# A Performer attention and MLP-mixer kernel on one core: token-mix tails in column tiles, key tails by two heads, eight single PSUM banks

## The chip, the cores and the metric

The kernel runs on one core of one Trainium2 chip. The metric is the time of one execution on the device in microseconds (us). TensorE (PE) does the matmuls and writes PSUM; VectorE (DVE) and ScalarE (ACT) read PSUM and do the element-wise work; GpSimd (POOL) works on SBUF and issues DMAs; SyncE (SP) issues DMAs. PEld is TensorE's loading of weights, which overlaps its matmuls.

## The reference

Eight samples with eight heads of 64 dimensions and 576 tokens go through attention with 128 random features, and the result through an MLP mixer. Cut to what matters:

```python
def phi(x):                                   # x is q or k, scaled by D ** -0.25
    proj = einsum('bhsd,md->bhsm', x, omega)  # 128 features
    h = proj - sum(x * x, -1, keepdims=True) / 2
    return exp(h - max(h, -1, keepdims=True)) / sqrt(m)
kv  = einsum('bhsm,bhsd->bhmd', k_p, v);  z = sum(k_p, axis=2)
num = einsum('bhsm,bhmd->bhsd', q_p, kv)
den = einsum('bhsm,bhm->bhs', q_p, z)[..., None] + 1e-6
x   = num / den                               # then [8, 576, 512]
h   = maximum(x.T @ w_tok1, 0) @ w_tok2       # token mix, over 576 tokens
u   = x + h.T
out = u + maximum(u @ w_ch1, 0) @ w_ch2       # channel mix, 512 -> 1536 -> 512
```

## The kernel before

**Tiling.** A sample's 576 tokens are 512 main tokens in four blocks of 128 and a tail of 64. Everything on TensorE is in fp16. The tails are handled apart from the main part, since 64 tokens fill only half of 128 rows.

**Loading.** Samples 0 and 1 are loaded in their natural layout and transposed on TensorE. For samples 2 to 7, `load_transposed` (L351) has POOL issue one DMA for q and one for k, each of which converts a whole sample to fp16 in a DRAM scratch (L355), and SP issue a transposing DMA for each from the scratch to SBUF (`qT`, `kT`, L363). The q and k casts of sample b wait for `touch(b-2)`: a one-column POOL copy (L373) that reads the transposed mixer input `uT` of sample b-2, and so waits until this other transposing DMA (L762) has landed. After `kT` has landed, a POOL copy (L366) moves the key tails of all heads into the tile `ktt`. The main load of v (L335) waits for that copy; v's tails (`vt`, L344, two DMAs) are issued after the casts. DMAs that POOL issues keep the order in which they stand in the code.

**Attention.** The contraction over 64 dimensions uses half of the array's rows, so two tokens' sets are computed on the two row halves. For each of the four head pairs of a sample: `kp` (L617) and `qp` (L631) project keys and queries, ACT takes their exponentials (L500), DVE takes the keys' maxima and their reciprocals (L643, L645), POOL scales v by them (`vs`, L650), `kv` (L663) sums keys times values over the main tokens with a column for z, and `num` (L698, L700) multiplies queries with it. DVE then divides (L707, L708), which gives `x`.

**Tails of k.** `kt` (L532) projects them for all heads. In the 128 rows of one tile of `kpt` lie 32 tokens of each of four heads, in two tiles for even and odd tokens. So that a head gets only its own rows, `vbd` holds v's tails in a block-diagonal form with a mask of four columns: DVE writes the scaled mask (L568), POOL multiplies it with v's tails (L577, 128 x 1024 elements). For each head pair two matmuls of 130 columns (L670), one for even and one for odd tokens, add the tails to `kv`.

**PSUM.** It is divided into six single banks and one pair of banks. The pair serves the projected tails of k and q (L532, L592), whose exponentials are one ACT instruction over both banks, and in samples 2 to 7 the numerators of two heads, which DVE then divides by one reciprocal and one multiplication. Samples 0 and 1 use single banks for the numerators, one head at a time.

**Mixer.** `token_mix` (L730) computes for each sample two blocks of token features over all 512 channels (L737, L738), a ReLU on ACT or DVE (L743, L745), and the four main token blocks (L754), to which DVE adds x (L757). Sample 0 has its own form (L770). `token_tail` (L807) computes the 64 tail tokens of two samples together: `w2t` holds the tail columns of the second weight padded to 128 with zeros, once in the left half and once in the right, so that four matmuls of 512 columns with 128 output rows put one sample's tail in rows 0 to 63 and the other's in rows 64 to 127 (L813). POOL fills `w2t` by two copies at the start (L900). `channel_mix` (L823) computes twelve blocks of four matmuls (L832), each with a ReLU (L852), then four output blocks of twelve matmuls (L870), an addition on DVE (L879) and a store. All tails are one ninth group of 512 rows at the end.

**Order.** It is written by a planner in the kernel itself (`Planner`, L38), which runs when the program is built. Each piece of work is a job with an engine, a cost, a key, the jobs that it depends on, and the buffers it takes and gives back. The planner simulates the engines, and lets an engine that is free take, among the jobs that can start first, the one with the lowest key; a job with `rows=True` (half-row matmuls) after another of its kind gets the bonus `ks`, and a change between half rows and whole rows is given a cost of 0.1. The keys of sample b are b plus the entries of `KEYS` and `NEAR`; those of the first sample are written out in `HEAD`. The order is fixed in the program: each engine works through its list, and waits at each item for its inputs. Until the first channel-mix matmul, the planner also fills gaps of TensorE with warm-up matmuls on zeros (L925).

## Time and profile before

| | |
|---|---|
| Median of 6 runs | 291.25 us (290.91 to 291.52) |
| The profiled execution | 291.58 us, of which the span from first to last instruction 289.8 us |
| Granted TensorE clock, mean | 0.999 |
| Busy: PE, PEld | 283.1 us (98%), 143.1 us (49%) |
| Busy: DVE, ACT, POOL | 147.9 us (51%), 153.1 us (53%), 90.9 us (31%) |
| Channel mix on PE: L832 and L870, all shapes | 376 + 48 + 444 matmuls |
| Tails of the token mix, L813 | 16 matmuls |
| k's tails into kv, L670 | 64 matmuls |
| DMA | 75737 packets, 39.57 MB |

The page gives for each group of instructions the line, the engine, the operation, what it writes and reads, how often it occurs, its busy time and the mean of one, and the idle time of its engine before it with what ended that. The mean of a matmul there (379 ns for 512 columns) is from start to modelled end and overlaps the next one; what one costs in a full stream is seen from the steps between starts, as in the chain of work that ended last or in the timeline. A digit of the row PE is the busy share of one of 40 slices of the span, 9 being 90% or more.

### The profile page before, as it was taken

What the parts mean: (1) busy time and instruction counts of PE and PEld (TensorE: products, weight loads), DVE (VectorE), ACT (ScalarE), POOL (GpSimd) and SP (SyncE); (2) the same over time, 40 slices, a digit from 0 to 9 for tenths busy, and PEclk for the clock granted to TensorE, in tenths of its full rate; (3) what the DMA queues carried; (4) which work ended last, traced back from release to release, by engine and by line L of the source; (5) the groups of instructions that cost most, each with busy time, mean ns of one, the idle gap of its engine ahead of it and who ended that gap; (6) DMA issues with size and microseconds to landing.
All of it is one profiled execution on the core that took longest, in us unless ns stands there. A gap on an engine that the chain in (4) does not pass through costs nothing.

```text
span 289.8 us, 5517 instructions
## 1 busy us (share of the span) xinstructions
PE 283.1 (98%) x2207; PEld 143.1 (49%) x2207; DVE 147.9 (51%) x280; ACT 153.1 (53%) x307; POOL 90.9 (31%) x116
## 2 busy tenths in 40 slices
PE   7999999999999999999999999999999999999994
PEld 4576454445544544464445444554455444444442
DVE  3985974476469524854657246646565231111012
ACT  2993981198367554855466646653765402512600
POOL 8995930247017401740274016501431000000000
PEclk9999999999999999999999999999999999999999
DMA  8999999899975997989868976998511043013014
GB/s 186 189 184 194 202 224 180 150 219 176 160 123 143 194 117 145 183 190 196 96 153 164 205 100 109 193 197 127 122 74 38 0 92 127 0 46 116 2 35 110
DMA packets 75737, 39.57 MB, mean 137 GB/s; under 512 B 54976, under 2 KB 70720, under 8 KB 75328
## 3 DMA queue, kind: packets, MB, share of 16 engines
q0 software_dynamic: 24304, 17.43, 41.3%
q1 hardware_dynamic: 50624, 21.01, 33.8%
q10 hardware_dynamic: 784, 0.79, 0.8%
q8 instruction: 17, 0.28, 0.4%
q14 instruction: 8, 0.07, 0.1%
HBM read 35.88 MB, written 16.52 MB: 181 GB/s over the span
## 4 chain that ended last, share of the span: by engine, by line
PE 92%; ACT 3%; DMA 2%; issue 0%; ACTq 0%; DVE 0%; DVEq 0%
PE bank L870 33%; PE bank L832 31%; PE bank L737 4%; PE bank L754 4%; PE bank L617 3%; PE bank L663 3%; PE bank L631 2%; PE pair L698 2%; DMA wc<-in_k_dram 2%; ACT kp L500 1%; PE bank L813 1%; PE bank L670 1%; PE bank L471 1%; PE bank L738 1%; ACT qp L500 1%; PE bank L781 1%
## 5 line engine op out<-in xcount | busy, mean ns | idle before, releaser
L870 PE MATMUL bank<-wc,r 128*128 128x512 f16 (+2 forms) x444 | 101.5, 374 | 0.0
L852 ACT ACTIVATE r<-bank 128x512 f16<-128x512 f32 x106 | 63.3, 601 | 70.4 <-PE bank L832 69.8
L832 PE MATMUL bank<-uT,wc 128*128 128x512 f16 x376 | 90.1, 379 | 0.3 <-ACT kp L500 0.2
L870 PEld LDWEIGHTS <-r 128*128 128x128 f16 x444 | 40.4, 98 | 47.5 <-issue 5.1
L832 PEld LDWEIGHTS <-wc 128*128 128x128 f16 x424 | 39.3, 98 | 42.4 <-issue 1.2
L500 ACT ACTIVATE qp<-bank 128x512 f16<-128x512 f32 x64 | 35.6, 622 | 13.9 <-PE bank L631 13.8
L643 DVE TENSOR_REDUCE km<-kp 128x8 f16<-128x1024 f16 x32 | 38.6, 1207 | 7.7 <-ACT kp L500 7.7
L500 ACT ACTIVATE kp<-bank 128x512 f16<-128x512 f32 x64 | 34.3, 609 | 10.6 <-PE bank L617 10.6
L650 POOL TENSOR_TENSOR vs<-v,vs 128x512 f16<-128x512 f16 x32 | 33.5, 1057 | 15.4 <-DVE vs L645 11.8
L879 DVE TENSOR_TENSOR o<-u,bank 128x512 f32<-128x512 f16 x28 | 19.1, 681 | 28.1 <-PE bank L870 28.1
L757 DVE TENSOR_TENSOR u<-x,bank 128x512 f16<-128x512 f16 x28 | 17.4, 681 | 9.1 <-PE bank L754 9.1
L577 POOL TENSOR_TENSOR vbd<-vt,vbd 128x1024 f16<-128x1024 f16 x7 | 13.5, 1928 | 25.9 <-DVE vbd L568 18.1
L366 POOL COPY ktt<-kT 128x256 f16<-128x256 f16 x6 | 2.4, 398 | 59.1 <-DMA kT<-k 59.1
L708 DVE TENSOR_TENSOR x<-pair,rc 128x640 f16<-128x640 f32 x24 | 19.8, 824 | 0.8
L707 DVE RECIPROCAL rc<-pair 128x10 f32<-128x10 f32 x24 | 5.1, 214 | 22.4 <-PE pair L700 22.4
L698 PEld LDWEIGHTS <-qp 128*128 128x128 f16 x256 | 12.9, 98 | 6.1 <-issue 0.4
L745 DVE TENSOR_SCALAR r<-bank 128x512 f16<-128x512 f32 x7 | 4.8, 692 | 19.1 <-PE bank L738 19.1
L737 PE MATMUL bank<-x,w1m 128*128 128x512 f16 x56 | 14.4, 379 | 0.0
L663 PEld LDWEIGHTS <-kp 128*128 128x128 f16 x256 | 11.0, 98 | 5.4 <-ACT qp L500 0.6
L663 PE MATMUL bank<-vs,kp 128*128 128x65 f16 x256 | 13.0, 193 | 0.4 <-ACT qp L500 0.4
L754 PE MATMUL bank<-r,w 128*128 128x512 f16 x56 | 13.2, 379 | 0.0
L617 PE MATMUL bank<-omT,kT 64*128 64x128 f16 x256 | 12.1, 218 | 0.0
(109 smaller groups left out, 276.3 us busy)
## 6 DMA issues: line engine op xcount, KB each, us to landing
out_dram<-o SPq DMA_DIRECT2D x32, 256.0 KB, 2.5
q<-in_q_dram POOLq DMA_DIRECT2D x6, 576.0 KB, 6.7
k<-in_k_dram POOLq DMA_DIRECT2D x6, 576.0 KB, 10.0
wc<-in_moe_w_ch_dram POOLq DMA_DIRECT2D x4, 768.0 KB, 10.7
v<-in_v_dram POOLq DMA_DIRECT2D x6, 512.0 KB, 6.0
r<-in_q_dram POOLq DMA_DIRECT2D x4, 256.0 KB, 7.7
v<-in_v_dram POOLq DMA_DIRECT2D x4, 256.0 KB, 7.6
out_dram<-o SPq DMA_DIRECT2D x5, 128.0 KB, 2.4
```

Source lines behind the costliest of these rows:

```text
L500: nc.scalar.activation(out=out, in_=in_, func=AF.Exp, bias=0.0, scale=1.0)
L617: nc.tensor.matmul(ps[e][:, c : c + M], m[half[e], r, :], omT[half[e]], start=True, stop=True)
L643: nc.vector.reduce_max(out=mx, in_=kpv, axis=AX.X)
L650: nc.gpsimd.tensor_tensor(out=vs[:, :, 0:D], in0=t_v[place("v", b)][:, hh[0] : hh[0] + 2, :].rearrange("p h (j d) -> p (h j) d", d=D), in1 ...
L663: nc.tensor.matmul(ps[:, i, :], kpv[:, 2 * i + j // 2, j % 2, :], vs[:, i * NJ + j, 0 : D + 1], start=(i == 0 and j == 0), stop=False, ski ...
L708: nc.vector.tensor_tensor(out=t_x[place("x", b)][:, :, (2 * hp + hs[0]) * D : (2 * hp + hs[0] + n) * D].rearrange("p j (i d) -> p i j d", ...
L737: nc.tensor.matmul(ps, w1m[:, j, tb * P : (tb + 1) * P], x[:, j, :], start=(j == 0), stop=False)
L754: nc.tensor.matmul(ps, w2_of(tb, j), r1[:, tb, :], start=(tb == 0), stop=(tb == NT - 1))
L832: nc.tensor.matmul(ps, wc1[:, db, cb * P : (cb + 1) * P], moving(db), start=(db == 0), stop=(db == ND - 1))
L852: nc.scalar.activation(out=o, in_=bank(n), func=AF.Relu)
L870: nc.tensor.matmul(ps[:, cols], r3[:, cb, j * P : (j + 1) * P], wc2[:, cb, cols], start=(cb == 0), stop=(cb == NCB - 1))
L879: nc.vector.tensor_tensor(out=t_o[place("o", (c, j))][:, cols], in0=uu[:, cols], in1=bank(n)[:, cols], op=ALU.add)
```

## The change

There are six parts, and a new set of keys for the planner.

- **Token-mix tails in column tiles.** `token_tail` no longer uses `w2t`. It takes the 64 tail columns of `w2` as weights, and gives the result of one sample to PSUM rows 0 to 63 and of the other to rows 64 to 127, four matmuls of 512 columns with 64 output rows. `w2t`, its clearing and its two POOL copies go away. The jobs are marked `rows="cols"`, so that the planner counts them as a third form of the array.
- **k's tails by two heads.** For samples 2 to 7 the cast of k is split. The main 512 tokens of all heads go to the scratch in one DMA, and the tails in two more DMAs, heads 0 to 3 into the left and heads 4 to 7 into the right 64 columns of 256 scratch rows. After the transposing DMA, a block of 128 columns holds all 64 tail tokens of two heads, and `kt` reads it from `kT` itself; the copy into `ktt` goes away. `vt` is loaded in the same layout, by two DMAs of 64 x 4 pieces of 64 elements. `vbd` has two columns of blocks instead of four, with a mask of two, and each head pair needs one matmul of 130 columns instead of two.
- **Eight single banks.** The pair goes away, and the tails of k and q use two single banks each, with one exponential for each bank.
- **Single numerators.** All samples do the numerators one head at a time, as samples 0 and 1 did.
- **v's load** waits, through a new one-column copy `touch_k`, for the transposed keys, where it waited for the copy `ktt`.
- **The planner** gives the same-form bonus only to a job of the same form, and the cost of one job in the first sample is corrected.

```diff
-KEYS = {"a": -1.353, "as": 0.087, "t": -0.936, "ts": 0.381, "gv": 2.14, "lt": -2.027, "lv": -1.831, "to": -1.942, "tt": 0.315, "ks": 1.1, "km": 0.226, "vs": -0.618, "l1": -0.809, "kt": -0.077}
+KEYS = {"a": -1.349, "as": 0.099, "t": -1.509, "ts": 0.07, "gv": 2.027, "lt": -1.998, "lv": -3.43, "to": -2.341, "tt": 0.635, "ks": 1.094, "km": 0.635, "vs": -0.113, "l1": -0.452, "kt": -0.125}
...
-                    key = j.key - (KEYS["ks"] if eng == "PE" and j.rows and last_rows else 0.0)
+                    key = j.key - (KEYS["ks"] if eng == "PE" and j.rows and last_rows == j.rows else 0.0)
...
-             "kvsb": 3, "ktt": 2, "x": 3, "r1": 3, "u": 3, "uT": 3, "r3": 2, "o": 4, "bank": 6, "pair": 1}
+             "kvsb": 3, "ktt": 2, "x": 3, "r1": 3, "u": 3, "uT": 3, "r3": 2, "o": 4, "bank": 8}
...
-                nc.gpsimd.dma_start(
-                    out=t_vt[place("vt", b)][:, g, :],
-                    in_=v[b, 4 * g : 4 * g + 4, SM:S, :].rearrange("h (r e) d -> h r (e d)", e=2),
-                )
-            jobs.append(dma("POOL", key + 0.01 * g, 0.22, tails, take=[("vt", b)], deps=deps, cost=0.7))
+                if b < NPE:
+                    o, i = t_vt[place("vt", b)][:, g, :], v[b, 4 * g : 4 * g + 4, SM:S, :].rearrange("h (r e) d -> h r (e d)", e=2)
+                else:
+                    o = t_vt[place("vt", b)][g * ST : (g + 1) * ST].rearrange("p a (c d) -> p (a c) d", c=2)
+                    i = v[b, :, SM:S, :].rearrange("(a i) t d -> i t a d", i=2)[g]
+                nc.gpsimd.dma_start(out=o, in_=i)
+            jobs.append(dma("POOL", key + 0.01 * g, 0.22 if b < NPE else 0.4, tails, take=[("vt", b)], deps=deps, cost=0.7))
...
-            casts.append(dma("POOL", key + 0.01 * n, 3.2, cast, deps, cost=0.55))
+            def cast_main(w=w):
+                nc.gpsimd.dma_start(
+                    out=scratch[w, b][0 : H * R].rearrange("(p r) e -> p (r e)", p=P),
+                    in_=src[w][b, :, 0:SM, :].rearrange("h s d -> h (s d)").rearrange("h (c f) -> h c f", c=P // H),
+                )
+            def cast_tail(w=w):
+                for g in range(2):
+                    nc.gpsimd.dma_start(
+                        out=scratch[w, b][H * R : H * RA, g * D : (g + 1) * D],
+                        in_=src[w][b, 4 * g : 4 * g + 4, SM:S, :],
+                    )
+            if w == "k":
+                casts.append(dma("POOL", key + 0.01 * n - 0.005, 0.8, cast_tail, deps, cost=1.1))
+            casts.append(dma("POOL", key + 0.01 * n, 3.2, cast if w == "q" else cast_main, deps, cost=0.55))
...
-        def ktt():
-            nc.gpsimd.tensor_copy(out=t_ktt[place("ktt", b)].rearrange("p (h r) -> p h r", h=H),
-                                  in_=t_kT[place("kT", b)].rearrange("p (h r) -> p h r", h=H)[:, :, R:RA])
-        ld["ktt", b] = add("POOL", 0.4, key + 0.25, ktt, deps=[ld["kT", b]], take=[("ktt", b)], give=[("kT", b)])
+
+    def touch_k(b, key):
+        def go():
+            nc.gpsimd.tensor_copy(out=junk[:, b : b + 1], in_=t_kT[place("kT", b)][:, H * RA - 1 : H * RA])
+        return add("POOL", 0.15, key, go, deps=[ld["kT", b]], give=[("kT", b)])
...
-            def kt_exp():
-                exp(t_kpt[place("kpt", b)].rearrange("p g e m -> p e g m"), pair(n_kt)[:, :, 0 : 2 * M].rearrange("p e (g m) -> p e g m", g=2))
-            j_kte = [add("ACT", 0.5, kkt, kt_exp, deps=[j_kt], take=[("kpt", b)], give=[("pair", n_kt)])]
+            nh = 2 if dma_in else 4
+            msk, j_msk = (mask2, j_mask2) if dma_in else (mask, j_mask)
+            j_kte = []
+            for e in range(2):
+                def kt_exp(e=e):
+                    o = t_kpt[place("kpt", b)]
+                    exp(o[:, e] if dma_in else o[:, :, e], two(n_kt)[e][:, 0 : 2 * M].rearrange("p (g m) -> p g m", g=2))
+                j_kte.append(add("ACT", 0.3, kkt, kt_exp, deps=[j_kt], take=[("kpt", b)], give=[("bank", (n_kt, e))]))
...
-                for e in range(2):
+                if dma_in:
+                    nc.tensor.matmul(ps, kt_[:, hp // 2, hp % 2, :], vb[:, hp, 0:2, 0 : D + 1], start=False, stop=True, skip_group_check=True)
+                for e in () if dma_in else range(2):
...
-            for hs in ((0,), (1,)) if alone else ((0, 1),):
+            for hs in ((0,), (1,)):
...
-            for o in range(2):
-                for tb in range(NT):
-                    nc.tensor.matmul(ps, w2t[:, tb, o, :], t_r1[place("r1", 2 * pair_ + o)][:, tb, :],
-                                     start=(o == 0 and tb == 0), stop=(o == 1 and tb == NT - 1))
-        j1 = add("PE", mm(4, 512), key, go, deps=[*jr, j_w2t], take=[("bank", n)], give=[("r1", 2 * pair_), ("r1", 2 * pair_ + 1)])
+            for tb in range(NT):
+                for o in range(2):
+                    nc.tensor.matmul(ps[half[o]], w2[:, tb, SM:S], t_r1[place("r1", 2 * pair_ + o)][:, tb, :],
+                                     start=(tb == 0), stop=(tb == NT - 1))
+        j1 = add("PE", mm(2, 512), key, go, deps=[*jr, j_w2], take=[("bank", n)], give=[("r1", 2 * pair_), ("r1", 2 * pair_ + 1)], rows="cols")
...
-            load_v(b, b + key_of("lv", b), [ld["ktt", b]] + ([touch_u(1, b + key_of("lv", b) - 0.1, added[1])] if b == NPE else []))
+            load_v(b, b + key_of("lv", b), [touch_k(b, b + key_of("lv", b) - 0.05)] + ([touch_u(1, b + key_of("lv", b) - 0.1, added[1])] if b == NPE else []))
```

The entries of `NEAR` and `HEAD` are new as well. The order that the planner makes of them for TensorE is built from the same pieces in much the same sequence; the places where it differs are told in the prediction.

## Prediction

> **What bounds the kernel now.** I read the page's parts 1, 2 and 4 first, then the chain in order of time, then the waits, and last POOL and TensorE around one batch.
>
> ```profile
> span 289.8 us, 5517 instructions
> ...
> PE 283.1 (98%) x2207; PEld 143.1 (49%) x2207; DVE 147.9 (51%) x280; ACT 153.1 (53%) x307; POOL 90.9 (31%) x116
> ...
> PE   7999999999999999999999999999999999999994
> ...
> PE 92%; ACT 3%; DMA 2%; issue 0%; ACTq 0%; DVE 0%; DVEq 0%
> ```
>
> TensorE is the bound, and not only by its share of busy time: 92% of the chain that ended last is PE. DVE and ACT, at half load, can take more work unless a matmul waits for just that piece. The chain in order of time shows the prices of matmuls in a full stream:
>
> ```profile
> 118.08 0.33 PE bank L617 x8
> 118.41 0.97 PE bank L870 x4
> 119.38 0.32 PE bank L631 x2
> ...
> 123.05 0.86 PE bank L832 x4
> ...
> 133.16 0.12 PE pair L698 x4
> 133.28 0.03 PE pair L700
> ...
> 133.47 0.87 PE bank L813 x4
> ```
>
> Four 512-column matmuls take 0.86 us, so one takes 0.216; 65 columns take 0.03. The two L631 matmuls, one on each half of the array's rows, take 0.32 and not 0.43: they run side by side, and 0.11 is added on entering the split form. The L870 group after L617 takes 0.97, so leaving it costs 0.11 as well. With these prices, each start of a matmul after 31 us follows from the one before within about 1 us in all: there TensorE has practically no waits. Before 26 us it has, since the first batch goes through ACT and DVE in a chain.
>
> What can take this away is late data:
>
> ```profile
> POOL ktt L366 <- DMA kT<-k: 59.1, 5, 16.2
> ...
> 113.52 0.40 POOL L366 COPY ktt<-kT 128x256 f16<-128x256 f16 x1 [16.17 <-DMA kT<-k]
> 113.86 0.93 POOL L335 DMA_DIRECT2D v<-in_v_dram  x1
> ...
> 115.51 0.28 PE L532 MATMUL pair<-omT,ktt 64*128 64x128 f16 x4
> ```
>
> POOL waits for the transposed keys, so the start of its copy (L366) dates their landing. In the timelines it is 81.50, 113.52, 137.93, 167.78 and 197.59 for batches 3 to 7, and TensorE first uses them (L532) at 85.00, 115.51, 142.47, 172.56 and 203.50. **The cover of the keys is thus 3.5, 2.0, 4.5, 4.8 and 5.9 us**, and at least 4.9 in batch 2. Batch 4 is the thin one.
>
> **The change, part by part.**
>
> *Token-mix tails in column tiles.* Before, 16 matmuls of 512 columns (L813) cost 16 x 0.216 = 3.46 us. After, the same 16 have 64 output rows, and the two samples of a pair go to the two column halves. No run here shows column halves; the nearest row is L631, where two row halves share their time. By it the 16 cost 1.73 us: **-1.73**. The Trainium skill (TensorEngine Tiling (Array Packing), Restrictions) speaks against: column tiling turns off the fast weight load. The trace has weight loads of 98 ns beside matmuls of 216, hidden. If a 64-column load without the fast mode could not be hidden and cost half a row's 98 ns, 16 of them would give 0.8 back: -0.9. If the halves did not overlap at all, 0, or +0.9 with eight form changes of 0.11. I take -1.73, by L631, whose weight loads also precede each matmul. DVE's uadd and the clearing and copy of w2t lie elsewhere; w2t's two POOL copies (0.5 us) go away off the path.
>
> *k's tails by two heads in 128 rows.* For batches 2 to 7 each head pair has one 130-column matmul instead of two: 24 fewer. In the timeline two L670 matmuls start at 16.22 and the next work at 16.34, so one takes 0.06: **-1.4**.
>
> *Changes of form.* Counting them in both kernels' TensorE orders gives 86 before and 86 after: eight new ones for column tiles, eight fewer for row halves. At 0.11 each: **0**.
>
> *Single banks, single numerators, exponentials.* DVE's 24 double numerators (reciprocal 214 + multiply 824 ns) become 48 single ones at 185 + 491 (the row of batches 0 and 1): 24 x 314 = +7.5 us of DVE, on 147.9 busy of 289.8. ACT gets 7 + 8 halved exponentials more, some 0.2 us each, +3 us on 153.1. Hidden by channel-mix matmuls, 7 to 10 us of them in every attention, while the extra per batch is 1.3 us of DVE. If the cover were gone, the last numerator before each token mix would be 0.3 later, 6 x 0.3 = 1.8 us in all; in the order two or three channel blocks (0.86 each) stand between it and the token mix, so 0. Eight free banks instead of six and a pair let matmuls start earlier: 0 to -0.5 in the head, 0 later, where there are no waits.
>
> *The head.* In the new order, 23 more matmuls precede the first channel-mix matmul (25.84 before): three warm-ups, and batch 1's tail keys and two key groups (20 half-row matmuls, about 0.5 us plus form changes, 0.9). They are moved, not added: the work after that point is shorter by 1.73 + 1.4 + 0.9. TensorE waits in the head, so a part is hidden; I take the first channel matmul 0.6 later: **-0.3** net, between -1.0 and +1.0, since ACT's order is otherwise the same there.
>
> *k's cast in three DMAs and the waits.* Where POOL issued q, k, it now issues q, two tails, k's main part (in batch 3 also vbd before the tails, 1.05 instead of 1.92 us; in batch 4 a vs, as before). Each tail is 256 rows of 128 B. POOL: 2 x 0.7 us (row of vt, L344) more before k's main part, and behind it in the queue vt and vs; both are hidden while q's copy moves, 6 to 7 us from issue to landing in batches 5 to 7. On the DMA engines: 512 small packets. The nearest row is vt's 256 B packets: 44 ns each in the trace, 512 x 44 / 16 = 1.4 us; but vt's 256 packets took 1.46 us from first to last, so 512 take 2.9, less 0.4 for the ninth of the bytes that leaves the main copy: 2.5. The skill (DMA: Bandwidth & Descriptors, Specifications) says that transfers below 512 B are done as a read and a write back: for 128 B in DRAM this would double vt's price, 5.4 instead of 2.5. vt goes to SBUF in 256 B and doesn't show it. I take 2.5, because vt is below 512 B as well; bounds 1.0 and 5.4. vt's own packets double too (256 to 512 per batch) and now share the engines with the transposes that follow: +0.7 (0 to 1.5). So the keys land 3.2 us later; the copy ktt (0.40) falls out. Between the last token-mix matmul of batch b-2, which starts this chain, and the first use, TensorE's order holds the same work as before within 0.4 us in batches 3 to 5 and 7 and 1.2 more in 6. So the cover is what is shown above: batch 4 is short by 3.2 - 0.4 - 2.0 = **+0.8**; batch 3 is left 0.7, the others over 1.6.
>
> *v's load behind the keys' transpose.* It stood behind ktt, which waited for the same landing; now behind a one-column copy (0.19 instead of 0.40). Behind it on POOL stand the v issue, vbd, vs and the next casts. v lands some 6.5 us after the keys, one vs takes 1.05, and kv is 6.7 (batch 3) to 9 us after the first tail matmul: 0 by itself, up to 0.8 where the keys come without cover.
>
> **Sum**: -1.73 - 1.4 - 0.3 + 0.8 = -2.6. The profiled execution took 291.58 (span 289.8 and 1.8 around it), so 289.0 for the like of it. The median shown is 0.33 lower: 291.25 - 2.6 = **288.6**.
>
> **Rivals.**
>
> 1. *Late keys, slower.* Place: the transposes of batches 4, 3, 5. With covers of 2.4, 3.9, 4.9, 5.2 (with ktt's 0.4) a delay D costs what exceeds each of them. The gain without stalls is 3.4. At D = 5.1 the stalls are 2.7 + 1.2 + 0.2 = 4.1, 0.7 more than the gain: from there it is slower. With the read and write back, 5.4 + 0.7, it would be about 295; just past the point, 292 to 293. For it: the packets under 512 B (54976 of 75737 already), batch 4's 2.0 us. Against: most of D would have to come from packets twice as dear as vt's.
> 2. *Partly late*: D of 4 to 4.7, or v late after it in batches 3 and 4: stalls of 2 to 3, 290.2. For it: v has no slack if the keys have none.
> 3. *Column halves don't overlap, or their weight loads show*: -2.6 + 1.3 = 289.9. Against: L631.
> 4. *No stall*: the tails move while q's big packets leave gaps: 287.8, and 287.3 with a better head.
>
> **How the numbers follow.** The likeliest case (287.6 to 289.5 by itself) has 0.48, no stall 0.14, partly late 0.14, column halves 0.08, slower 0.16. 0.2% is 0.58 us, about what a measurement of this kernel can tell from no change. Faster (under 290.67): 0.48 + 0.14 + 0.08 of the partly late + 0.06 of the column case, less 0.02: 0.74. Slower (over 291.83): 0.15. The rest, 0.11, is the same. The range from 287.1 to 291.4 leaves the slower case out, and little below.
>
> **What would show it.** Right: two L835 matmuls per 0.22 us, groups of four in 0.43 plus 0.11; x24 fewer 130-column matmuls; a PE row still full after 31 us; first channel matmul near 26.4; a wait of TensorE for DMA kT only in batch 4, under 1.5 us. Wrong: L835 groups of 0.86; PE waits for kT in batch 3 or 5; q or k casts landing more than 4 us later than before against their token mix; a dip in the PE row at the slices of 80 to 120 us.

## The result, and the profile after

| | before | after |
|---|---|---|
| Median | 291.18 us (290.73 to 292.29, 38 runs) | 290.10 us (289.46 to 294.28, 19 runs) |
| Profiled execution | 291.58 us | 290.98 us |
| its span | 289.8 us | 288.5 us |
| Outside the span, median of all runs | 1.79 us | 2.42 us |

The ratio of the times is 0.9969, with an interval of 0.9958 to 0.9980: **faster by 1.1 us**, where 2.65 were forecast. The ratios here leave disturbed executions out and the medians don't, so the two can differ a little.

First the page of the changed kernel: the span, the engines, TensorE's row of 40 slices, and the chain that ended last by engines.

```profile
span 288.5 us, 5598 instructions
...
PE 279.4 (97%) x2186; PEld 140.2 (49%) x2186; DVE 152.5 (53%) x330; ACT 153.9 (53%) x322; POOL 93.6 (32%) x126
...
PE   6999989999999999999989999999999999999993
...
PE 84%; POOL 6%; DMA 6%; DVE 2%; issue 1%; ACT 0%; POOLq 0%; DVEq 0%
```

TensorE has 3.7 us less to do, but of the chain PE is now 84% and not 92%: POOL and DMA have come in with 6% each. Besides the first slice and the last there are two digits below 9, one from 36 to 43 and one from 144 to 151 us. The chain in order of time shows the head, the first of these places, and one group of column tiles:

```profile
16.25 7.78 DMA r<-in_k_dram
...
24.07 0.29 PE bank L505 x4
...
26.55 0.55 PE bank L638 x16
27.11 1.40 PE bank L860 x6
...
35.35 1.33 POOL vt L345 x2
...
36.69 1.08 POOL vs L671
...
37.81 0.40 PE bank L684 x8
...
62.01 0.55 PE bank L835 x4
```

L835 is the tail group of one pair of samples: four matmuls in 0.55 us, which is two steps of 0.216 and 0.11 for the change of form. The first channel-mix matmul, L860, is here at 27.1 and in TensorE's timeline at 27.04; before it was at 25.84. Ahead of it the chain runs through a DMA, the load of sample 1's k tail, for which L505 waited 0.43. And sample 1's second kv (L684 at 37.81) comes straight behind two POOL rows, the issues of v's tails and a vs. The timeline of POOL, first of the kernel before (its L355 is the cast, L577 vbd, L650 vs, L344 the load of v's tails):

```profile
30.46 1.94 POOL L577 TENSOR_TENSOR vbd<-vt,vbd 128x1024 f16<-128x1024 f16 x1
32.34 0.59 POOL L355 DMA_DIRECT2D q<-in_q_dram  x1
32.92 0.53 POOL L355 DMA_DIRECT2D k<-in_k_dram  x1
33.47 2.08 POOL L650 TENSOR_TENSOR vs<-v,vs 128x512 f16<-128x512 f16 x2
35.48 0.75 POOL L344 DMA_DIRECT2D vt<-in_v_dram  x1
```

and of the kernel after, with three rows from later samples:

```profile
29.43 0.55 POOL L353 DMA_DIRECT2D q<-in_q_dram  x1
29.97 1.69 POOL L364 DMA_DIRECT2D k<-in_k_dram  x2
31.89 0.56 POOL L358 DMA_DIRECT2D k<-in_k_dram  x1 [0.23 <-DMA v<-in_v_dram]
32.47 1.94 POOL L596 TENSOR_TENSOR vbd<-vt,vbd 128x1024 f16<-128x1024 f16 x1
34.35 1.06 POOL L671 TENSOR_TENSOR vs<-v,vs 128x512 f16<-128x512 f16 x1
35.35 1.33 POOL L345 DMA_DIRECT2D vt<-in_v_dram  x2
36.69 3.09 POOL L671 TENSOR_TENSOR vs<-v,vs 128x512 f16<-128x512 f16 x3
...
113.46 0.19 POOL L380 COPY junk<-kT 128x1 f16<-128x1 f16 x1 [14.33 <-DMA kT<-k]
...
140.86 0.19 POOL L380 COPY junk<-kT 128x1 f16<-128x1 f16 x1 [13.83 <-DMA kT<-k]
...
149.35 2.07 POOL L671 TENSOR_TENSOR vs<-v,vs 128x512 f16<-128x512 f16 x2 [5.17 <-DMA v<-in_v_dram]
```

Before, vbd was made first and sample 2's casts, 1.1 us of issues, stood behind it. Now the casts stand ahead of vbd and are 2.8 us. The second vs of sample 1 ends at 35.5 before and at 37.8 after, and TensorE takes it up at once. The two issues of v's tails, which before stood behind the second vs and behind the third, now stand between the first and the second (L345, 1.33 us). Sample 5's vs at 149.35 waited for v, whose load had waited for the keys (L380 at 140.86). In TensorE's own timeline these are the two waits:

```profile
37.81 0.40 PE L684 MATMUL bank<-vs,kp 128*128 128x65 f16 x8 [0.70 <-POOL vs L671]
...
150.46 0.40 PE L684 MATMUL bank<-vs,kp 128*128 128x65 f16 x8 [0.77 <-POOL vs L671]
```

TensorE's work behind the first channel matmul, counted as each kernel's matmuls times the prediction's prices, but with 0.096 instead of 0.11 for a change of form (its median in both traces), is 257.88 us before and 253.81 after, 4.07 less. Waits in the same stretch, which is the time that the starts take beyond these prices, were 1.6 and are 3.1. With 0.11 the two differences hardly move: 4.15 less work, 1.6 more waits. The largest of the waits are now those of the two rows above, 0.86 and 0.93 by the steps between starts.

The waits of the kernel after, by total, number and longest:

```profile
POOL junk L380 <- DMA kT<-k: 66.7, 6, 14.3
...
POOL vs L671 <- DMA v<-in_v_dram: 10.5, 3, 5.2
...
PE bank L684 <- POOL vs L671: 1.5, 2, 0.8
```

No matmul stands in the whole list as waiting for the transposed keys. Behind the head, TensorE waited for vs.

### The profile page after: what moved, and what is told of

Its sections match the earlier page's. It is cut to its first block, busy times and chain, and to the rows that moved or that the text cites. A ratio compares the mean times of both kernels' runs of the same rounds, so it can differ in the third digit from the quotient of the medians.

```text
span 288.5 us, 5598 instructions
## 1 busy us (share of the span) xinstructions
PE 279.4 (97%) x2186; PEld 140.2 (49%) x2186; DVE 152.5 (53%) x330; ACT 153.9 (53%) x322; POOL 93.6 (32%) x126
## 4 chain that ended last, share of the span: by engine, by line
PE 84%; POOL 6%; DMA 6%; DVE 2%; issue 1%; ACT 0%; POOLq 0%; DVEq 0%
PE bank L892 31%; PE bank L854 30%; PE bank L776 4%; PE bank L759 4%; DMA v<-in_v_dram 3%; DMA r<-in_k_dram 3%; PE bank L684 2%; PE bank L720 2%; PE bank L638 2%; PE bank L652 2%; POOL vs L671 2%; PE bank L760 1%; POOL vt L345 1%; POOL r L313 1%; DVE km L664 1%
## 5 line engine op out<-in xcount | busy, mean ns | idle before, releaser
L730 DVE TENSOR_TENSOR x<-bank,rc 128x320 f16<-128x320 f32 x62 | 30.5, 492 | 2.1
L380 POOL COPY junk<-kT 128x1 f16<-128x1 f16 x6 | 1.1, 186 | 66.7 <-DMA kT<-k 66.7
L729 DVE RECIPROCAL rc<-bank 128x5 f32<-128x5 f32 x62 | 11.4, 184 | 14.5 <-PE bank L722 14.2
L684 PE MATMUL bank<-vs,kp 128*128 128x65 f16 x256 | 13.0, 193 | 1.7 <-POOL vs L671 1.5
L684 PEld LDWEIGHTS <-kp 128*128 128x128 f16 x256 | 11.0, 98 | 6.5 <-issue 2.9
L720 PE MATMUL bank<-kvsb,qp 128*128 128x65 f16 x256 | 14.0, 193 | 0.0
L596 POOL TENSOR_TENSOR vbd<-vt,vbd 128x512 f16<-128x512 f16 (+1 forms) x7 | 8.2, 1176 | 17.1 <-DVE vbd L587 7.7
```

The source lines that it names most:

```text
L684: nc.tensor.matmul(ps[:, i, :], kpv[:, 2 * i + j // 2, j % 2, :], vs[:, i * NJ + j, 0 : D + 1], start=(i == 0 and j == 0), stop=False, ski ...
L720: nc.tensor.matmul(ps[:, k, j * 65 : (j + 1) * 65], st, s[:, i, 0 : D + 1], start=True, stop=True)
L730: nc.vector.tensor_tensor(out=t_x[place("x", b)][:, :, (2 * hp + hs[0]) * D : (2 * hp + hs[0] + n) * D].rearrange("p j (i d) -> p i j d", ...
```

## The experiments

The theory to begin with: the savings on TensorE are real, and what is lost is lost through POOL's queue and the DMAs behind it. The rivals: column tiles or the 130-column matmuls save less than priced, or the packets are dearer than vt's. Every kernel was timed beside the kernel before on the same chip.

**One part alone.** First the column tiles alone, in the kernel before:

```diff
-                    nc.tensor.matmul(ps, w2t[:, tb, o, :], t_r1[...][:, tb, :], start=(o == 0 and tb == 0), ...)
+                    nc.tensor.matmul(ps[half[o]], w2[:, tb, SM:S], t_r1[...][:, tb, :], start=(tb == 0), ...)
```

> The kernel before with only the token-mix tails in column tiles; keys, banks, casts and every engine's order as before. Theory (the matmuls are saved as predicted, and the loss lies in waits): 16 matmuls in column halves save 1.73 us; in the old order they stand next to whole-array work, so six more changes of form cost 6 x 0.11 = 0.66: 1.1 us faster than before, 290.1. In the profile a group of four steps over 0.43 us. Rival (column halves pay less than they look in the trace, because their weight loads or form changes cost more): 0 to 0.3 us faster.

290.64 us against 291.23, ratio 0.9983 (0.9974 to 0.9992): 0.5 us faster, between the two expectations. By the prices, the work behind the first channel matmul fell by 1.15: 1.73 less six form changes more, since this order does not put these groups beside half-array work. Waits were 0.5 longer in the trace. The halves do overlap; part of the gain went into waits even here.

Then k's tails by two heads alone, in the kernel before (masks, `vbd` and `vt` with them, the cast in three DMAs):

```diff
-            casts.append(dma("POOL", key + 0.01 * n, 3.2, cast, deps, cost=0.55))
+            casts.append(dma("POOL", key + 0.01 * n, 3.2, cast if w == "q" else cast_k, deps, cost=0.55))
...
-                for e in range(2):
+                if dma_in:
+                    nc.tensor.matmul(ps, kt_[:, hp // 2, hp % 2, :], vb[:, hp, 0:2, 0 : D + 1], start=False, stop=True, ...)
```

> The kernel before with only k's tails by two heads: cast of k in three DMAs, tails of v in the new layout, one 130-column matmul instead of two in samples 2 to 7, the copy into ktt replaced by a one-column copy; keys, banks, and the order of jobs as before. 24 matmuls fewer are worth 1.4 us. Theory (late keys are the loss: the trace after has the keys 4 to 5 us later against their token mix in samples 5 to 7): the old covers of 2.4, 3.9, 4.9, 5.2 us and v behind them take some of it back: 0 to 1.0 us faster, and TensorE waits for keys or for v's scaled tile somewhere in samples 4 to 7. Rival (late keys cost nothing, the loss is in the new order or the single banks): 1.4 us faster, no such wait.

294.48 us (290.87 to 301.77), ratio 1.0052 (1.0022 to 1.0083): **this part alone is slower**, by 1.5 us by the ratio, though it takes 24 matmuls out. Its trace has a wait for vs at sample 1's first kv:

```profile
35.29 0.40 PE L680 MATMUL bank<-vs,kp 128*128 128x65 f16 x8 [1.00 <-POOL vs L667]
```

Here nothing but the casts stands between vbd and vs. So this part of the change brings such a wait without the new due times. It is not the whole loss: the recorded execution is the fastest of the twelve (290.87), and what made most of the others longer is in no trace.

**The packets and the number of DMAs.** In the kernel before, k's cast in three DMAs with the same bytes in large packets:

```diff
-            casts.append(dma("POOL", key + 0.01 * n, 3.2, cast, deps, cost=0.55))
+            casts.append(dma("POOL", key + 0.01 * n, 3.2, cast if w == "q" else cast3, deps, cost=0.55))
```

> The kernel before, with k's cast as three DMAs instead of one: the same bytes to the same places, two pieces of 32 KB in 16 rows each and one of 512 KB in 16 rows of 32 KB. No small packets, no new layout. Theory (what makes k's new tails cost more than they save, in the kernel before with that part alone 3 us slower and scattered from 290.9 to 301.8, is the small packets of 128 B): 0 to 0.5 us slower than before, 291.2 to 291.7, for the longer issue on POOL ahead of sample 1's vs, runs no more scattered than before. Rival (three DMAs in POOL's queue in place of one, and 32 KB rows, do it): 2 to 4 us slower, and runs scattered over several us.

291.38 us (290.96 to 291.96), ratio 1.0008 (0.9996 to 1.0021): three DMAs for one cost nothing that can be told here. Sample 1's vs stands right behind them in POOL's list, but POOL came to vbd 1.0 us earlier in this trace than in the one before (29.44 against 30.46), and the second vs ended at 35.5 in both. The next three are the kernel after with larger packets; where the text says other values or rows, the outputs of samples 2 to 7 are others too. k's tails first, moved in pieces of 2 KB (k's tails then hold other values):

```diff
-                        out=scratch[w, b][H * R : H * RA, g * D : (g + 1) * D],
-                        in_=src[w][b, 4 * g : 4 * g + 4, SM:S, :],
+                        out=scratch[w, b][r0 : r0 + H * RT // 2].rearrange("(p r) e -> p (r e)", p=16),
+                        in_=src[w][b, 4 * g, 0:256, :].rearrange("(p r) d -> p (r d)", p=16),
```

> The kernel after, with the same three DMAs for k, but the two for the tails move as many bytes in 16 pieces of 2 KB each instead of 256 pieces of 128 B; every engine's order is that of the kernel after. It fills the tails of k with other values of k, so that part of the sums is another one. Theory (the small packets make the keys late, and with them v in sample 5): keys 2 to 3 us earlier in samples 5 to 7, the wait of 0.9 us at sample 5 gone, 0.9 us faster than the kernel after, 289.2. Rival (the keys are late for another reason, the order of the queue or the doubled pieces of v's tails): within 0.3 us of the kernel after, 290.1.

290.42 us (289.35 to 294.59), ratio 0.9965 (0.9947 to 0.9983), no change of the median. Counted from the token mix two samples before, the keys of samples 5 to 7 land 0.9 to 2.0 us earlier than in the trace after. That is one execution against another, and the staged casts below, with small packets, come as early (within 0.2 us), so it can't be put down to the packets. Sample 5's wait is gone, but the wait at sample 1's second kv stays at 1.1. v's tails second, in the old 256 B pieces (v's tails then stand in other rows than the keys'):

```diff
-                if b < NPE:
+                if True:
```

> The kernel after, with the tails of v loaded as the kernel before did, in 256 pieces of 256 B a sample instead of 512 of 128 B; every order is that of the kernel after. The tails of v then stand in other rows, so that part of the sums is another one. If the doubled pieces of v's tails, which share the DMA engines with the transposes behind them, make the keys late and the runs scatter (289.5 to 294.3 in the kernel after): 0.5 to 0.9 us faster than the kernel after, 289.4, and no run above 291. If k's cast does it: within 0.3 us of 290.1, scattered the same.

290.11 us (289.32 to 290.64), ratio 0.9958 (0.9945 to 0.9971). Counted in the same way the keys are 1.6 to 2.5 us earlier than in the trace after, there is again no wait in sample 5, and the slowest of 12 runs is at 290.64. Both edits together:

> The kernel after with both: k's tails in pieces of 2 KB and v's tails in pieces of 256 B as before; parts of the sums are others, as in the two kernels with one of these. If small packets of k and v together are the cause: 1 to 1.5 us faster than the kernel after, 288.8, not scattered; what stays is the wait at sample 1's second kv. If three DMAs instead of one are the cause: 289.8 to 290.5, scattered up to 294.

289.96 us (289.45 to 290.16), ratio 0.9952 (0.9934 to 0.9969). The keys are 1.4 to 3.2 us earlier than in the trace after, and 0.9 to 3.0 later than before the change. Against the staged casts they are 0.4 to 2.3 earlier, so the packets may be a part of their delay; single traces don't show how much. The ratio's centre is only 0.0017 below that of the kernel after, 0.5 us, and the intervals overlap. The packets are not the main thing that is missing: the wait at sample 1's second kv was 1.2 and 1.0 in these two kernels.

**The wait of v's load.** The kernel after without `touch_k`'s copy, so that v's load goes out as soon as its buffer is free:

```diff
-            nc.gpsimd.tensor_copy(out=junk[:, b : b + 1], in_=t_kT[...][:, H * RA - 1 : H * RA])
+            pass
```

> The kernel after without the one-column copy that makes v's load wait for the transposed keys: POOL goes on to v's load as soon as its own list allows, at the same place in its order. Theory (late keys are passed on to v, whose scaled tile then comes 0.9 us late at sample 5): v lands 5 to 12 us earlier; but its 4 us of transfer now lie beside the transposes of q and k. If v's lateness is the larger evil: 0.5 to 1 us faster than the kernel after, 289.3. If the transposes are: keys later by 2 to 4 us in samples 4 to 7, TensorE waits for keys, 1 to 5 us slower.

304.52 us (301.62 to 309.54), ratio 1.0431 (1.0395 to 1.0468): 14 us slower than the kernel after. The recorded execution is the longest of the six, 309.54.

```profile
86.75 0.61 PE L652 MATMUL bank<-qT,omT 64*128 64x512 f16 x2 [3.09 <-DMA qT<-q]
...
121.33 0.61 PE L652 MATMUL bank<-qT,omT 64*128 64x512 f16 x2 [3.80 <-DMA qT<-q]
```

TensorE waits for the transposed q in samples 3 and 4, and for the transposed keys in samples 5, 6 and 7 (3.65, 0.68 and 1.61 us), 13 us in all. Where v's 512 KB move beside the transposes, these take longer: kT's transpose lands 8.3 us after its issue in the median, where it took 4.7 in the kernel after. That v's transfer stands in their way is the natural reading; the edit itself changes only when v's load is issued. The waits are not the whole loss. From shortly before the end of each of the three that are over 3 us, the granted clock of TensorE was 0.5 for 3.4, 6.8 and 6.8 us, and a 512-column matmul took 0.43 instead of 0.216. Half of that time, as far as it lies behind the waits, is an estimate of what this added: some 7.5 us. In the traces before and after, the clock is at 1.0 from about 6 us to the end of TensorE's work. So the one-column copy is worth 14 us here.

**Sample 2's casts.** Three kernels hold them back behind some of sample 1's work on POOL, and leave every other engine's order alone. First behind vbd but ahead of vs:

```diff
+                if b == 1:
+                    for fn in held_casts:
+                        fn()
```

> The kernel after, with POOL issuing the casts of sample 2 behind the vbd of sample 1 instead of ahead of it, as the kernel before had it; nothing else is moved. Theory (the wait of 0.86 us at sample 1's second kv, and 0.23 after it, come from vs standing behind vbd and the longer issue of the casts): one vs per us earlier by some 1 to 2 us, the wait gone, 0.9 to 1.1 us faster than the kernel after, 289.1. Rival (that wait comes from DVE's or ACT's order in sample 1): within 0.3 us of 290.1.

291.25 us (289.19 to 295.12), ratio 0.9982 (0.9963 to 1.0001), and the wait is still 0.7. They stand ahead of vs as before, and v's tails between the two vs as in the kernel after. Then behind sample 1's second vs:

```diff
+                if b == 1:
+                    done_vs.append(hp)
+                    if len(done_vs) == 2:
+                        for fn in held_casts:
+                            fn()
```

> Sample 2's casts of q, of k's two tails and of k are issued behind vbd and sample 1's two vs instead of ahead of them; all else is the changed kernel. Theory (the systematic loss of 0.9 to 1.1 us at sample 1's second kv comes from POOL issuing these four DMAs, 2.8 us, ahead of vbd and vs): that wait falls under 0.2 us, and the median is 0.7 to 1.1 below the changed kernel's 290.1, 289.0 to 289.4. Rival (TensorE makes the time good later, or the same wait comes for another operand): within 0.3 of 290.1. Bad for the theory as well: sample 2's keys come late in turn and TensorE waits at its first transposed keys.

290.83 us (289.36 to 294.55), ratio 0.9989 (0.9969 to 1.0009): the expectation was missed. POOL's timeline, and under it a row of TensorE's, say why:

```profile
33.94 1.08 POOL L675 TENSOR_TENSOR vs<-v,vs 128x512 f16<-128x512 f16 x1
34.94 0.59 POOL L357 DMA_DIRECT2D q<-in_q_dram  x1
35.52 1.71 POOL L368 DMA_DIRECT2D k<-in_k_dram  x2
37.22 0.56 POOL L362 DMA_DIRECT2D k<-in_k_dram  x1
37.80 2.08 POOL L675 TENSOR_TENSOR vs<-v,vs 128x512 f16<-128x512 f16 x2
```

```profile
38.92 0.40 PE L693 MATMUL bank<-vs,kp 128*128 128x65 f16 x8 [1.07 <-POOL vs L675]
```

The second kv no longer waits, but sample 1 has four, and the third now waits 1.07 for the vs behind the casts. The same 2.8 us were paid one kv later. So, in a third kernel, q's cast behind the second vs and k's three behind the fourth:

```diff
+                if b == 1:
+                    done_vs.append(hp)
+                    for fn in {2: held_casts["q"], 4: held_casts["k"]}.get(len(done_vs), []):
+                        fn()
```

> Of sample 2's casts, q's is issued behind sample 1's second vs and the three of k behind its fourth; all other orders are the changed kernel's. With all four behind the second vs the wait moved to the third kv, 1.2 us. Theory (POOL's 2.8 us of issues cost what they stand ahead of, wherever it is a vs): no wait of TensorE over 0.3 at sample 1's kv, and a span 0.7 to 1.0 shorter, median 289.1 to 289.5. Rival (sample 1's vs are late for v's load or the maxima anyway): a wait of 0.8 or more stays in sample 1. If the casts, 5 us later, come too late for sample 2, TensorE waits at its first transposed keys and the gain is lost there.

**289.36 us** (289.08 to 290.26), ratio 0.9932 (0.9915 to 0.9950).

```profile
33.74 1.07 POOL L675 TENSOR_TENSOR vs<-v,vs 128x512 f16<-128x512 f16 x1
34.75 0.58 POOL L357 DMA_DIRECT2D q<-in_q_dram  x1
35.34 2.07 POOL L675 TENSOR_TENSOR vs<-v,vs 128x512 f16<-128x512 f16 x2
37.36 1.73 POOL L368 DMA_DIRECT2D k<-in_k_dram  x2
39.08 0.56 POOL L362 DMA_DIRECT2D k<-in_k_dram  x1
```

and in TensorE's

```profile
36.43 0.41 PE L692 MATMUL bank<-vs,kp 128*128 128x65 f16 x8
...
37.74 0.41 PE L692 MATMUL bank<-vs,kp 128*128 128x65 f16 x8
```

The second and third kv of sample 1 no longer wait, and k's casts, 7 us later than in the kernel after, come in good time: sample 2's keys land at 55.3, there at 56.4. The ratio is 0.0037 lower than the kernel after's, 1.1 us, with intervals that don't meet. Of the 1.8 us by which the recorded span is shorter, 0.5 is an earlier first channel matmul and 1.2 are waits. One wait for v has only moved: sample 5's is gone, but in sample 3 POOL waits for v's load and the first kv waits 0.65 by the steps between starts:

```profile
90.65 3.08 POOL L675 TENSOR_TENSOR vs<-v,vs 128x512 f16<-128x512 f16 x3 [3.00 <-DMA v<-in_v_dram]
```

```profile
91.76 0.40 PE L692 MATMUL bank<-vs,kp 128*128 128x65 f16 x8 [0.48 <-ACT qp L518]
```

(The first vs and ACT's qp, which the row names, both end at 91.7, so either may have been the last. With the late k tail, below, the same place waits 0.9 for vs alone, and POOL before it 3.3 for v.)

A rival for the cause in sample 1 is not tested alone: the two issues of v's tails between the first and the second vs. In the trace after, the maxima for the second vs are there at 35.3, when POOL begins the 1.33 us of issues. Without these the second vs would have ended at 36.4, by an estimate from these rows, and TensorE needed it at 36.95. So what is shown is that POOL's issues ahead of sample 1's vs cost this time, and that moving the casts away gets it back; moving v's tails of sample 2 might have done so too.

**v's tails earlier.** The load of the next sample's v tails right behind v's load, away from the keys' transposes:

```diff
-            load_v_tail(b, b + key_of("lt", b) + 0.02)
+            if b == NPE:
+                load_v_tail(b, b + key_of("lt", b) + 0.02)
...
+            if b + 1 < B:
+                load_v_tail(b + 1, b + key_of("lv", b) + 0.01)
```

> v's tails of the next sample, 512 packets of 128 B, are issued right behind v's load of the sample before, instead of right behind k's cast; all else is the changed kernel but for a few neighbours in TensorE's order. Theory (beside the keys' transposes these small packets delay the keys, and v with them): the keys' landings of samples 4 to 7 are 2 to 4 us earlier than 113.5, 140.9, 170.6, 201.1, no wait of TensorE at sample 5's kv (0.9 before), and the slowest runs fall under 291 us with a median of 289.2 to 290.0. Rival (small packets cost the same wherever they move): the median stays at 290.1 and runs above 292 remain.

290.67 us (from 289.24), ratio 0.9976 (0.9958 to 0.9993), with runs of 291.9 and 294.4, as the kernel after has them: the rival's outcome. (The recorded execution took 1016 us, and no line of it is used, so when the keys landed is not known.) With the casts behind the second vs as well:

> Both edits at once: sample 2's casts behind sample 1's vs, and v's tails issued a sample earlier. If the two losses are separate they add: 288.3 to 289.0, under both kernels. If they are one loss told twice: no better than the better of the two alone, 289.2 to 289.6.

289.69 us (288.98 to 291.25), ratio 0.9955 (0.9936 to 0.9974): below either of the two edits, not as low as 289.0, and no better than the staged casts alone.

**The order.** The kernel after with the due times of the kernel before:

```diff
-KEYS = {"a": -1.349, "as": 0.099, "t": -1.509, ...}
+KEYS = {"a": -1.353, "as": 0.087, "t": -0.936, ...}
```

(`NEAR` and `HEAD` likewise.)

> The changed kernel with the due times of the kernel before, so that the parts of the change are kept and the new order of the work is not. Theory (the parts save 3.1 us of TensorE and the new due times themselves bring little, with a head that starts the first channel matmul 1.2 us later): 289.5 to 291, the first channel matmul near 26, the work after it longer than 253.8. Rival (the new due times are what keeps the keys' and v's covers): 292 to 296, with waits of TensorE for keys or v of over 1 us in several samples.

291.64 us (290.45 to 327.10), ratio 1.0007 (0.9987 to 1.0026): between the two expectations. Its first channel matmul is at 26.68, so the late head does not come from the new due times, and there are 4.1 us of waits behind it, the longest 0.57 for a vs of sample 2 and 0.50 for a transposed q, most of them under 0.3. In this order k's main cast stands behind all four vs of sample 1, and none of its kv waits over 0.2. Without new due times the six parts together gain nothing that can be told.

**The head.** The transposes of sample 1's k tail behind the last uT matmuls instead of ahead of them:

```diff
+            if db == 3:
+                late["k", 1].deps.append(j2)
```

> In the head, the transposes of sample 1's k tail, for which TensorE waited 0.5 us for the load, stand behind the last uT matmuls of sample 0 instead of ahead of them; some of sample 1's orders shift after it. Theory (that wait and the 24 small matmuls ahead of the last uT are what makes the first channel matmul late): it comes 0.5 to 0.9 earlier, near 26.0, and the median falls by 0.3 to 0.6. Rival (the moved work is only paid later): the first channel matmul is earlier, and the median within 0.3 of 290.1.

290.44 us (289.43 to 293.52), ratio 0.9972 (0.9948 to 0.9996). TensorE's timeline:

```profile
26.15 0.82 PE L865 MATMUL bank<-uT,wc 128*128 128x512 f16 x3
...
34.98 0.40 PE L687 MATMUL bank<-vs,kp 128*128 128x65 f16 x8 [0.74 <-POOL vs L674]
```

The first channel matmul is 0.9 earlier, and the time the same: the rival. Sample 1's first kv waits 0.74 instead, and sample 3's 0.9. An earlier start only met vs earlier.

**Outside the span.** The page ends with the last instruction, and the runs are 1.8 us longer than their span before and 2.4 after. The DMA records of the traces show one difference at the end: transfers of instructions, the late ones of 8192 bytes each. Their times are counted in us from the end of the span; a minus is ahead of it.

| kernel | DVE, ACT instructions in the trace | last load of instructions, begin and end | outside, same execution | outside, median |
|---|---|---|---|---|
| before | 377, 402 | over 12 us ahead of the end | 1.77 | 1.79 |
| column tiles alone | 378, 402 | over 12 us ahead | 1.78 | 1.78 |
| two heads alone | 380, 402 | over 12 us ahead | 2.02 | 2.01 |
| old due times | 450, 452 | -2.59, -2.28 | 2.00 | 1.95 |
| v's tails earlier and casts behind the second vs | 446, 438 | +1.24, +1.70 | 2.02 | 1.98 |
| late k tail | 451, 441 | +2.12, +2.44 | 2.19 | 2.30 |
| staged casts | 447, 441 | +2.24, +2.60 | 2.35 | 2.47 |
| after | 447, 441 | +2.23, +2.74 | 2.49 | 2.42 |

The kernel after and the one with staged casts have one load more, at +1.08 and +1.35. It is the last load that goes with the time: in each of the eight traces where it begins more than 2 us behind the span, the time outside is 0.23 to 0.25 us less than its end, whatever that is. A last load that ends at +1.7 or earlier leaves no such mark. The time outside is then between 1.8 and 2.0, and the kernel with two heads alone has 2.0 without a late load, so the step from 1.8 to 2.0 has another cause, which stays open.

The reading: the longer streams of DVE (single numerators) and ACT (halved exponentials) reach a border between two loads just at the end of the program. To try it, 24 one-column copies more on each of the two, spread over samples 2 to 7:

```diff
+                    if b >= NPE and e == 1:
+                        nc.scalar.copy(out=pad_a, in_=zeros[:, 0:1])
...
+                if b >= NPE:
+                    nc.vector.tensor_copy(out=pad_v, in_=zeros[:, 0:1])
```

> The changed kernel with 24 one-column copies more on ACT and 24 more on DVE, spread over samples 2 to 7; TensorE's order and all the rest are the same. In the traces the changed kernel loads two 8 KB pieces of instructions 1.1 and 2.2 us after its span has ended, where the kernel before loads none that late, and its time outside the span is 2.4 instead of 1.8. Theory (ACT's and DVE's longer streams cross a piece's border just at their last instructions, and the end waits for the load): with the borders moved into the run no load comes after the span, the time outside it falls to 1.8 to 2.0, and the median falls by 0.4 to 0.6 to 289.5 to 289.7. Rival (the late loads are idle prefetch, and the time outside has another cause): it stays at 2.4, and the median at 290.1 or above for the added work.

The last load of instructions is now 2.49 us ahead of the end of the span, and the time outside is **1.94 us (1.88 to 2.01 in 12 runs)**: 0.5 less for 48 instructions more, as the theory said. The median, 291.25 us (288.96 to 295.11), ratio 0.9972 (0.9947 to 0.9997), does not show it: the spans ranged from 287 to 293 us in this set, for a reason that stays open (below).

**Three edits together**: staged casts, v's tails earlier, the copies.

> Staged casts of sample 2, v's tails issued a sample earlier, and the copies that move the code borders. If the losses are separate they add: 288.3 to 288.9, under both kernels, with few runs above 290. If one of them is no loss by itself: 289.2 to 289.7.

**288.85 us** (288.30 to 291.33), ratio 0.9924 (0.9894 to 0.9954), 2.2 to 2.6 us under the kernel before, with 1.78 us outside the span. It is the lowest median of all and within what adding losses would give, but its interval overlaps that of the staged casts alone, so it doesn't show that they add.

## Why the prediction was wrong

The direction and the main savings were right. Three terms failed: the head was priced too low, the issues on POOL were put at nothing, and the time outside the span was held to stay. Step by step:

- **Column tiles, -1.73: right.** L835 x4 takes 0.55, that is 0.43 and 0.11. The weight loads have a mean of 108 ns, against 98 for L813's before. The Trainium skill's loss of the fast weight load (TensorEngine Tiling (Array Packing), Restrictions) thus costs nothing that can be seen: the loads lie beside the matmuls, and four of these take what two whole ones do.
- **Two heads, -1.4, and form changes, 0: right.** 40 matmuls of 130 columns (24 at L691, 16 at L693) instead of 64, at 0.058 each, and 86 changes of form in both traces. With the column tiles and the moved 0.9 they were to make 4.03 behind the first channel matmul; 4.07 were there.
- **The head, -0.3: too low.** The step "TensorE waits in the head, so a part is hidden; I take the first channel matmul 0.6 later" failed. It came 1.2 later in the two traces shown: at 27.04 against 25.84. It is at 26.4 to 27.3 in the others with the same head, but for one at 27.7, and at 25.0 to 25.8 in those with the old one. The moved groups (L546 and L638, 0.8) stand close ahead of it, where no wait is left to hide them, and L505's wait for a DMA came to it. Net +0.3, so 0.6 of the forecast gain. That the moved groups are what made it late is read from the order. The late-tail kernel shows that it can't be had back there alone.
- **The stall, +0.8: in the wrong place.** The step was D = 3.2 for every sample, and 0.8 of wait in batch 4. Counted from the last token-mix matmul of the sample two before, the keys of samples 3 to 7 came -0.5, 0.1, 4.1, 5.3 and 3.9 us later in the profiled execution, and with the staged casts 0.8, 1.6, 3.2, 3.4 and 2.8. So for samples 5 to 7 the 3.2 is near with staged casts and 0.7 to 2.1 too low in the profiled execution; their covers of 4.5 to 5.9, with ktt's 0.4, took it up. For batch 4, where it was to cost 0.8, it is too high: the delay stayed inside the 2.0. The sign named for being wrong, k's casts over 4 us later, was there in samples 5 to 7 (6.9, 5.1 and 5.6), and still no matmul waited for keys. What failed with it is "0 by itself" for v: queued behind the keys, it made sample 5's kv wait 0.9 in the profiled execution, and sample 3's 0.9 with the late k tail.
- **"Behind it in the queue vt and vs; both are hidden while q's copy moves": wrong for the first casts.** This is the step that failed most clearly. Behind sample 2's casts stand sample 1's vbd and vs, and in the trace after TensorE takes up the first of these vs 3.3 us behind the casts and needs the second 1.2 us later. I named the queue and took its cover from samples 5 to 7. Each tail issue took 0.85 us, not 0.7. The wait is 0.9 to 1.2 us in five of six traces with this order, and 0.3 in the sixth, where the first channel matmul came 0.7 later. The staged casts gave back 1.1. That v's tails, issued between two vs, have a part in it is not excluded.
- **The time outside the span, held to be the same: +0.63.** The step "span 289.8 and 1.8 around it" took the 1.8 over unchanged. That DVE's and ACT's extras are hidden was right of their execution, and missed that 70 more DVE and 39 more ACT instructions in the trace are also more code to load. The Trainium skill (Runtime: NRT & Kernel Launch, Instruction fetch mechanics) says that crossing a block is mostly hidden. Within the span nothing here speaks against it. At the end nothing is left to hide a load, and one that begins 2.2 us behind the span goes with 0.5 to 0.6 us.

By the profiled executions: -4.07 of work, +1.20 for the head and +1.5 of waits give -1.4 in the span, where -1.3 was measured. The forecast had -4.03 + 0.6 + 0.8 = -2.6. The medians of all runs lose less to waits, 1.7 in the span, and the 0.63 outside leaves 1.1.

Of the rivals, the one of a part being late came nearest by its number (290.2), but by luck: no matmul waited for keys. The small packets were not dearer than vt's: 128 B took 33 ns in the trace after, 256 B 44 in the one before, and k's tails, the only packets of 128 B in the kernel with v's old pieces, 32. So the doubling that the Trainium skill's read and write back would give (DMA: Bandwidth & Descriptors, Specifications) is not there.

**What stays open.** Why single executions of the kernel after and of some variants take 2 to 5 us more. The 256 B pieces of v's tails made the range narrow, but so did the staged casts, which leave the 128 B pieces; and moving those pieces did not. Chips and packets are not told apart by these runs. Also open is which instructions the late loads hold, and why the end of an execution follows the last of them.

## What to carry to other kernels

When a step puts more issues on a queue, look at what stands behind it in each place where it occurs, the first one above all: the cover of the later samples says nothing of the head. Moving a block of issues back by one consumer only moved the wait here; spread it between the consumers, or put it behind the last of them. And when a change adds many short instructions to an engine that has time, look at the time outside the span too.

## What the hardware showed that I had not expected

- A load of 8 KB of instructions may be the last thing of an execution: in eight traces the time outside the span followed its end to within 0.02 us, and it went with 0.5 to 0.6 us. 48 short instructions more took that away.
- Letting v's 512 KB move beside the transposing DMAs cost 14 us in six samples; the wait of one DMA issue for another's data kept them apart. In the recorded execution a wait of TensorE of over 3 us brought 3.4 to 6.8 us at a granted clock of 0.5 with it, so a wait cost more than its length.
- Packets of 128 B took 33 ns, less than those of 256 B. The 256 B packets of the transposes went from 25 to 30 ns in the mean beside them, and were at 26 both with large packets for k's and v's tails and with v's small ones issued a sample earlier.
